# Pairwise adds and residual adds as accumulating DMAs in a fused attention and GeGLU block

## The chip, the cores and the metric

The kernel runs on one core of a Trainium2 chip. The metric is the device time of one execution in microseconds (us). Three executions of the kernel before gave 184.48, 184.34 and 184.0 us, so a median of 184.34 us.

## What is computed

The input is a bf16 activation x of 2048 rows (tokens) and 512 columns. The output is x plus the output of an attention branch plus the output of a feed-forward branch, both fed with a layer norm of x that has no scale or bias.

```
xn  = layernorm(x)                                   # 2048 x 512
q, k, v = xn @ wqkv                                  # 32 heads of 16 columns each
logit[h, s, w] = sum_d q[h,s,d] * k[h,s-2w,d] / 4    # w = 0..7, a dilated window of 8 keys
attn = softmax over w (keys before the start masked)
o[h, s, d] = sum_w attn[h,s,w] * v[h,s-2w,d]
out = x + o @ wo + (gelu(xn @ w_gate) * (xn @ w_up)) @ w_down      # 1376 inner columns
```

## The kernel before

The 2048 tokens are cut into four blocks of 512. In the code they have the numbers b = 0 to 3; the text calls them block one to block four. Tokens also come in sixteen tiles of 128 rows, four to a block. Activations are held transposed: a partition is a column of x, and the 512 tokens of a block lie along the free axis. Columns of wqkv are picked with a stride, so that a partition holds four groups (g = 0 to 3) of 512 tokens, and the 16 columns of one head are spread over four neighbouring partitions and the four groups.

For each block the work goes through these steps.

1. Layer norm of the block's tiles. For blocks one and two VectorE does it with ScalarE's square root; for blocks three and four ScalarE does the sums, GpSimd a power (L832, one operation for two tiles) and VectorE a reciprocal (L803). Blocks two to four are transposed by DMA transposes from SyncE's queue (L882, called SP in the profile).
2. Projections on TensorE, 128x512 matmuls in groups of four: q, k and v (L1009, names mm), gate and up (L1217, names fg and fu). ScalarE moves the results out of PSUM, with the tanh form of GELU for the gate.
3. Logits. VectorE multiplies q with eight shifted views of k: four products of 128x4096, one for each group (L1040, names pr). Two adds of 128x4096 (L1053, names pa) bring them to two: product 0 + 1, and product 2 + 3. The rest of the sum over d is done by TensorE against a matrix E8 that adds four partitions and scales: the task er (L1073 to L1094), which also holds 16 small matmuls for the last up columns (L1078). For both remaining products it issues 8 matmuls (L1085), four of which side by side fill the four 32-row strips of a PSUM bank.
4. Softmax over the window. VectorE takes the maximum (L1117) and subtracts it (L1122), ScalarE the exponential (L1131), VectorE sums, takes the reciprocal (L1138 to L1150) and multiplies (L1155). The probabilities go to a scratch in HBM by four stores (L1164) and come back spread over the partitions of a head by four loads (L1176).
5. Values. VectorE makes four products of 128x4096 (L1184, names pv), three adds (L1193, names pw) and a last add of the two halves (L1199, name pz), which gives the transposed attention output.
6. Feed-forward. VectorE multiplies the GELU with the up projection (L1241 and L1279, names h).
7. Output, for each tile of 128 tokens: 4 matmuls with wo and 11 with w_down into one bank (L1302, names acc). For tiles 0 to 13 ScalarE copies the bank to an SBUF buffer OB (L1335, names fe), VectorE adds the tile of x (L1340, names fin), which SP had loaded into a buffer XR (L1288, names ldxr), and SP stores OB (L1353, names sto). The last two tiles are cut into two and three column parts, and VectorE adds from PSUM (L1346). There are two XR and four OB buffers.

Every instruction or DMA is a task of a graph, with what it reads and writes. The dictionary ORDER (L404 to L461) writes out by hand, for each of the five engines, in which order its tasks are issued. The function schedule (L207) replays these orders with assumed durations, only to hand out buffers of the pools; assign_sync (L317) gives each task a semaphore and finds the waits; emit_engine (L364) issues the tasks in the order written. Each engine works strictly in its order, so a task at the head that waits holds up all behind it.

The parts that the change touches: PR_ADD3 (L512) is empty in the kernel before. For blocks that it names, a third pairwise add is made at L1060 to L1063, and the reduction issues the E8 matmuls for one product only (hhs at L1071, L1082). The tuple FIN2 (L511) names the tiles of step 7 that take ScalarE's copy and VectorE's residual add from SBUF.

Of the kernel before, what the change touches and what calls it, by code (L numbers as in the profile page):

```python
# [12 lines left out]
    DMA_ISSUE=0.48,  # L13
    DMA_FIXED=2.0,
# [5 lines left out]
    DRAIN=0.1,  # L20
# [115 lines left out]
class Graph:  # L136
# [70 lines left out]
    def schedule(self, orders, params=None):  # L207
# [59 lines left out]
        for _ in range(len(self.tasks)):  # L267
# [23 lines left out]
            elif t.eng == "pe":  # L291
                sw = 0.0
                if t.mode is not None:
                    if pe_mode not in (None, t.mode):
                        sw = prm["PE_MODE_SWITCH"]
                    pe_mode = t.mode
                t.end = est + sw + pe_clock.run(est, t.dur, t.util)
                t.done = t.end + prm["PE_DRAIN"]
            else:
                t.end = est + t.dur  # L300
                t.done = t.end + prm["DRAIN"]
                if t.eng == "act" and t.table is not None:
                    act_table = t.table
# [13 lines left out]
    def assign_sync(self, cnt_sems, dma_sems):  # L317
        order = self.order
        for e in ("pe", "act", "dve", "pool"):
            for i, t in enumerate(order[e]):  # L320
                t.seq = i + 1
                t.sem = cnt_sems[e]
                t.val = i + 1
        dcount = [0] * len(dma_sems)
        dlast = [None] * len(dma_sems)
        k = 0
        for t in order["sp"]:
# [6 lines left out]
            dlast[si] = t  # L334
        self.dma_totals = [(dma_sems[i], dcount[i]) for i in range(len(dma_sems)) if dcount[i] > 0]
        know = {e: {} for e in ENGS}
        allt = sorted((t for t in self.tasks if not t.dropped), key=lambda t: (t.start, t.idx))
        for t in allt:
            K = know[t.eng]
            deps = list(t.deps)  # L340
            if t.eng == "sp" and t.prev_on_sem is not None:
                deps.append(t.prev_on_sem)
# [21 lines left out]
    def emit_engine(self, eng_name, e):  # L364
# [7 lines left out]
        for t in self.order[eng_name]:  # L372
# [4 lines left out]
            if eng_name == "sp" and t is self.order["sp"][-4]:  # L377
                late = self.order["sp"][-7:]
                for (s, tot) in self.dma_totals:
# [3 lines left out]
            ins.then_inc(t.sem, 16 if eng_name == "sp" else 1)  # L383
# [5 lines left out]
    def report(self):  # L389
# [17 lines left out]
        "warm14 mma0_0 tpx0_1 mmt0_0 mmt0_1 mmt1_0 tpx1_0 mmt1_1 mmt0_2 tpx1_1 mmt1_2 mmt0_3 mmt1_3 "  # L407
        "mm0_2_0_0 mm0_2_3_0 mm0_2_2_0 mm0_2_1_0 fg0_0 fg0_1 fg0_2 fu0_0 fg0_3 fu0_1 fu0_2 fg0_4 fu0_3 fg0_5 "
        "fu0_4 fu0_5 fg0_6 fg0_7 er0_3 mm1_0_0_0 mm1_1_0_0 mm1_0_1_0 mm1_1_1_0 fg1_0 fu0_6 mm1_0_3_0 "
        "mm1_0_2_0 mm1_1_3_0 fu0_7 fu1_0 fg1_1 fg0_8 fu1_1 mm1_1_2_0 fu0_8 mm1_2_0_0 fg1_2 fg0_9 fu1_2 "  # L410
        "mm1_2_2_0 fg1_3 fu1_3 fu0_9 fg0_10 fg1_4 fu1_4 mm1_2_3_0 fg1_5 mm1_2_1_0 fg1_6 fu1_5 fu1_6 fg1_7 "
        "mm2_0_0_0 mm2_1_1_0 mm2_1_0_0 mm2_0_3_0 er1_3 mm2_0_1_0 fg1_10 mm2_1_2_0 mm2_2_1_0 mm2_0_2_0 fu1_7 "
        "fg2_0 accd1 mm2_1_3_0 accd2 fg2_1 mm2_2_3_0 mm2_2_2_0 fg1_8 fg2_2 acca0 fu2_0 accb0 fg1_9 mm2_2_0_0 "
        "accd3 er2_3 fu2_1 fu1_8 fu1_9 fu2_2 fg2_3 fu2_3 mm3_1_2_0 mm3_1_1_0 mm3_1_3_0 mm3_0_1_0 mm3_0_0_0 "
        "fg2_4 mm3_1_0_0 fu2_4 mm3_0_2_0 fg3_0 mm3_0_3_0 fu3_0 fg3_1 fg2_10 fg3_2 accd7 accd5 mm3_2_0_0 "
        "fg2_5 fu3_1 fg3_3 mm3_2_3_0 mm3_2_1_0 fu2_5 fu3_2 acca4 er3_3 accb4 fg3_4 accd6 fu3_3 fu3_4 fg2_6 "
        "fg3_5 fu2_6 fg2_7 fg3_6 fu2_7 fg2_8 fu2_8 fu3_5 fg3_7 fu3_6 mm3_2_2_0 fg2_9 fu3_7 fu2_9 fg3_8 fu3_8 "
        "fg3_9 fg3_10 acca8 accd10 accd9 fu3_9 accb8 accd11 acca12 accd13 accd14_0 accd14_1 accw14_0 "
        "accw14_1 accw13 accb12 accd15_0 accw12 accw15_0 accd15_1 accw15_1 accd15_2 accw15_2",
    "act":  # L420
        "c_tbl sx1 sq0 negm1 sxx1 sq1 evx0_0 evx0_1 evq0_0 sq2 evq0_1 evk0_0 evx1_0 sq3 evk0_1 bnst8 evx1_1 "
        "bnst9 evq0_2 sq6 evk0_2 evq0_3 evk0_3 ve8 evv0_0_0 sq4 vp8 bnag8 bnag9 va8 gelu0_0 evv0_2_0 "
        "evv0_3_0 bnst10 gelu0_1 bnst11 uev0_2 gelu0_3 vb8 gelu0_4 uev0_1 uev0_3 ve10 gelu0_5 uev0_4 uev0_0 "
        "uev0_5 gelu0_2 halo1 vp10 gelu0_7 bnag10 bnag11 evq1_0_0 evk1_0_0 evv0_1_0 evq1_1_0 evk1_1_0 "
        "gelu0_6 exp0 sub11 evq1_3_0 evk1_3_0 evq1_2_0 va10 uev0_7 uev1_0 uev0_10c uev0_6 sub9 vb10 sub8 "
        "uev1_1 evk1_2_0 norm9 uev0_10b gelu1_1 gelu1_0 norm8 gelu0_8 evv1_0_0 gelu1_2 sub10 uev0_8 bnst12 "
        "gelu0_9 norm11 uev1_2 uev0_9 norm10 evv1_2_0 gelu1_4 gelu1_3 uev1_3 evv1_1_0 uev1_4 uev1_5 uev0_10a "
        "bnst13 gelu1_5 gelu0_10 uev1_6 evk2_1_0 evv1_3_0 evk2_0_0 ve12 vp12 gelu1_7 bnag12 evq2_0_0 gelu1_6 "
        "evq2_1_0 uev1_10b bnag13 uev1_10c halv1 evk2_2_0 evq2_2_0 halo2 exp1 bnst14 sub12 bnst15 uev1_7 "
        "va12 ve14 vb12 uev1_10a vp14 bnag14 evk2_3_0 bnag15 evq2_3_0 evv2_1_0 va14 vb14 fe1 fe2 sub14 "  # L430
        "gelu2_0 evv2_2_0 halo3 gelu1_10 sub15 uev2_0 norm12 sub13 evv2_0_0 evv2_3_0 norm13 fe0 norm15 fe3 "
        "norm14 gelu1_8 gelu2_1 gelu1_9 uev2_1 uev1_8 uev2_2 uev1_9 uev2_3 gelu2_2 evk3_2_0 evk3_1_0 "
        "uev2_10b gelu2_3 exp2 evq3_1_0 evk3_3_0 evq3_2_0 evq3_0_0 halv2 evk3_0_0 uev2_10c evq3_3_0 uev2_4 "
        "uev2_10a gelu2_10 gelu3_1 uev3_0 gelu3_0 fe7 evv3_0_0 gelu2_5 gelu3_3 evv3_1_0 uev2_5 uev3_1 fe5 "
        "gelu2_4 gelu3_2 uev3_10c halv3 evv3_3_0 uev3_2 fe4 fe6 uev3_3 uev3_10b exp3 gelu3_5 uev2_6 gelu3_4 "
        "gelu2_7 uev2_7 uev2_8 gelu3_6 gelu2_6 evv3_2_0 gelu3_7 uev3_4 gelu2_8 gelu2_9 uev2_9 uev3_10a "
        "uev3_7 uev3_5 uev3_6 gelu3_10 fe10 gelu3_8 gelu3_9 uev3_9 fe9 uev3_8 fe8 fe11 fe13 fe12",
    "dve":
        "c_wdz bnst0 bnag0 sub0 rstd0 norm0 mean1 sub1 evy0_0 rstd1 norm1 evy0_1 bnst2 bnag2 sub2 rstd2 "
        "norm2 bnst3 bnag3 sub3 rstd3 norm3 bnst7 bnst6 bnst5 bnag6 bnag7 bnst4 bnag5 sub7 rstd6 bnag4 sub6 "  # L440
        "norm7 sub4 sub5 norm6 pr0_2 pr0_0 pr0_3 rstd4 pr0_1 norm4 norm5 pa0_1 pa0_0 h0_0 h0_1 h0_2 mask "
        "d1_0 d2_0 pr1_0 pr1_1 d4a_0 d4b_0 d4c_0 d5_0 rstd8 d6_0 pr1_3 pa1_0 pr1_2 h0_3 pa1_1 pv0_1 rstd10 "
        "pv0_3 h0_4 pv0_0 h1_1 pv0_2 pw0_1 h0_10 pw0_2 d1_1 pw0_3 d2_1 pz0 pr2_2 d4a_1 pr2_0 d4b_1 h1_3 "
        "d4c_1 h1_2 d5_1 h1_0 d6_1 pr2_1 pr2_3 pa2_0 fin1 rstd12 pa2_1 h1_10 pv1_1 rstd14 pv1_3 d1_2 pv1_0 "
        "d2_2 pv1_2 pw1_1 fin3 pw1_2 h2_1 pw1_3 h1_4 d4a_2 pz1 d4b_2 pr3_1 d4c_2 pr3_2 d5_2 fin0 d6_2 pr3_3 "
        "pr3_0 h2_0 h2_10 pa3_0 fin2 pa3_1 pv2_0 pv2_2 d1_3 pv2_1 d2_3 pw2_1 h3_1 d4a_3 h3_0 d4b_3 fin7 "
        "d4c_3 h2_2 d5_3 fin5 d6_3 pv2_3 pw2_2 h2_3 pw2_3 h2_4 pz2 fin4 pv3_3 pv3_0 pv3_1 fin6 pw3_1 fin10 "
        "h3_3 h3_10 pv3_2 h3_2 fin9 h3_4 pw3_2 fin8 pw3_3 fin11 pz3 fin14_0 fin14_1 fin13 fin15_0 fin15_1 "
        "fin12 fin15_2",
    "pool":  # L450
        "c_ones c_onef c_id c_vnpad c_idb c_eps c_mhalf c_e8a c_e8b c_e8c c_e8d c_ktpad c_mask0 c_mask1 "
        "c_utz sq8 sq10 sq12 sq14",
    "sp":
        "ld_x0_0 ld_x0_1 ld_wq ld_x1_0 ld_wk ld_x1_1 ld_wv ld_x2 ld_x4 ld_x3 ld_wg0 ld_wu0 ld_wt0 ld_x5 "
        "ld_wt1 trx3_0 ld_wt2 trx3_1 trx2_0 trx2_1 ld_wd0 ld_x6 ldxr1 ld_x7 ld_wd1 ld_wo ss0_2 ss0_3 ss0_0 "
        "ss0_1 ldxr2 sl0_1 sl0_3 sl0_2 trx4_0 sl0_0 trx4_1 trx5_1 trx5_0 ss1_2 ss1_3 ss1_1 ss1_0 sl1_1 sl1_3 "
        "sl1_0 sl1_2 ldxr3 trx6_0 trx6_1 trx7_1 trx7_0 sto3 sto1 ldxr0 ldxr7 ss2_1 ss2_2 ss2_3 ss2_0 sl2_0 "
        "sl2_3 sl2_2 sto0 sl2_1 sto2 ldxr5 ldxr4 sto5 ss3_0 ss3_1 ss3_2 ss3_3 ldxr10 sl3_3 sl3_0 sl3_2 sl3_1 "
        "ldxr6 sto4 sto6 ldxr8 ldxr9 sto9 ldxr11 ldxr14 sto8 sto7 sto10 ldxr13 sto11 sto14_0 sto14_1 ldxr15 "
        "ldxr12 sto13 sto15_0 sto15_1 sto12 sto15_2",  # L460
# [20 lines left out]
def bass_parallel_sum__sliding_local_dilated__glu_gated_geglu__prompt_kernel(nc, A_x, A_wqkv, A_wo, B_x, B_w_gate, B_w_up, B_w_down, out, dbg=None, cfg=None):  # L481
# [28 lines left out]
    PPOW = cfg.get("PPOW", 4)  # L510
    FIN2 = cfg.get("FIN2", tuple(range(14)))  # L511
    PR_ADD3 = cfg.get("PR_ADD3", ())  # L512
# [11 lines left out]
    with contextlib.ExitStack() as es:  # L524
# [56 lines left out]
        cnt = {e: es.enter_context(nc.semaphore("cnt_" + e)) for e in ("pe", "act", "dve", "pool")}  # L581
        dsems = [es.enter_context(nc.semaphore("dma%d" % i)) for i in range(NDMASEM)]
# [360 lines left out]
        for b in range(NB):  # L943
# [94 lines left out]
            for g in range(4):  # L1038
# [21 lines left out]
                if g == 3 and b in PR_ADD3:  # L1060
                    t_of["pa%d_2" % b] = G.task(
                        "dve", "pa%d_2" % b, d_dve(4096, 0.52), mk_pa(pr_items[0], pr_items[2]),
                        rd=[pr_items[2]], wr=[pr_items[0]], prio=base + 20.2)  # L1063
# [218 lines left out]

            for ti in range(4):
                t = 4 * b + ti
                it_xr = Item("xr%d" % t, P_xr, "xr")

                def mk_xr(t=t, it=it_xr):
                    return lambda e: e.dma_start(XR[:, it.slot, :], x2[128 * t:128 * t + 128, :])  # L1288
                t_xr = G.task("sp", "ldxr%d" % t, 0, mk_xr(), wr=[it_xr], prio=base + 58, nbytes=128 * 1024)
                G.order_after(t_xr, t_of["gelu%d_5" % b])  # L1290
# [47 lines left out]

# [78 lines left out]
```

## Time and profile before

| what | value |
|---|---|
| median of three runs | 184.34 us |
| the profiled execution: its own time | 184.58 us |
| the profiled execution: its span in the profile | 182.7 us |
| granted TensorE clock | 1.0 throughout |
| third pairwise add of the logit products | none |
| L1085 reduction matmuls | 64, 16 in each block |
| L1340 residual adds, 128x512 | 14, mean 416 ns |
| L1053 pair adds, 128x4096 | 8, mean 2286 ns |
| DMAs from GpSimd | none |

The profile is of one execution. PE is TensorE's matmuls and PEld its weight loads, DVE is VectorE, ACT is ScalarE, POOL is GpSimd, SP is SyncE, SPq the issuing of DMAs on its queue. The chain of work is followed back from the last instruction, at each step to what released it or to the instruction before it on its engine; each piece has a start, a length, and the engine and line. A timeline has a start, a length, the engine and line, the operation, output and input tiles, and at the end, in brackets, idle time before it and what ended it. Durations overlap: a VectorE operation begins before the one ahead has drained, so what an operation costs its engine is read from start to start. In a table of stretches each engine has its busy time and instructions in the stretch, then come the granted clock, the mean busy share of the 16 DMA engines and the GB/s that they moved.

### The profile page before, as it was taken

The page shows a single profiled execution, that of the slowest core. Times are in us where ns is not written, and L with a number is a line of the kernel's source. Part 1 is how long each engine was busy: PE and PEld are TensorE (multiplying, and loading weights), DVE is VectorE, ACT ScalarE, POOL GpSimd, SP SyncE. Part 2 cuts the span into 40 slices and gives each one's busy share as a digit, 9 for nine tenths or more (in the row PEclk, how much of TensorE's full clock was granted, in tenths as well). Part 3 has the DMA queues.
Part 4 walks back from the last instruction along what each step waited for, and adds up shares of the span by engine and source line. Part 5 has one row for each costly group of instructions (what it writes and reads, how often), then busy time and mean ns, then how long its engine had stood idle before and what let it go on. Part 6 is the DMA issues. An engine that isn't in the chain of part 4 may idle for free.

```text
span 182.7 us, 2790 instructions
## 1 busy us (share of the span) xinstructions
PE 178.9 (98%) x1068; PEld 90.6 (50%) x1068; DVE 169.6 (93%) x172; ACT 128.4 (70%) x258; POOL 9.5 (5%) x23
## 2 busy tenths in 40 slices
PE   8999999999999999999999999999999999999994
PEld 2886444544444444444444544444444444444664
DVE  3769999999999999999999999999999999999922
ACT  5688987999999899998695977527449764234011
POOL 6000010003300000122000000000000000000000
PEclk9999999999999999999999999999999999999999
DMA  4999905932562000002851020128000346022433
GB/s 125 360 376 381 125 18 118 367 127 49 183 145 57 0 0 4 0 12 76 256 62 30 4 82 0 30 62 285 28 0 0 92 131 213 0 86 61 140 104 100
DMA packets 26221, 19.60 MB, mean 107 GB/s; under 512 B 13825, under 2 KB 23009, under 8 KB 26209
## 3 DMA queue, kind: packets, MB, share of 16 engines
q1 hardware_dynamic: 26208, 19.44, 37.0%
q8 instruction: 8, 0.13, 0.3%
q14 instruction: 5, 0.03, 0.1%
HBM read 14.71 MB, written 3.15 MB: 98 GB/s over the span
## 4 chain that ended last, share of the span: by engine, by line
PE 91%; DMA 4%; SPq 2%; ACT 1%; issue 0%; DVE 0%; DVEq 0%
PE PS L1217 38%; PE PS L1302 28%; PE PS L1009 19%; DMA XIN<-in_A_x_dram 4%; PE PS L1256 2%; PE PS L1085 2%; PE PS L1078 1%; PE PS L959 1%; SPq L731 1%; SPq L687 1%; ACT XS L769 0%; SPq L737 0%; ACT xnT L919 0%; DVE OB L1346 0%; DVEq L376 0%
## 5 line engine op out<-in xcount | busy, mean ns | idle before, releaser
L1302 PE MATMUL PS<-Wd,HT 128*128 128x512 bf16 (+2 forms) x209 | 41.0, 346 | 0.0
L1217 PE MATMUL PS<-xnT,Wg 128*128 128x512 bf16 x160 | 39.8, 379 | 0.0
L1217 PE MATMUL PS<-xnT,Wu 128*128 128x512 bf16 x160 | 39.1, 379 | 0.0
L1009 PE MATMUL PS<-xnT,Wqkv 128*128 128x512 bf16 x160 | 38.0, 380 | 0.0
L1184 DVE TENSOR_TENSOR UNI<-VN,PT 128x4096 f16<-128x4096 bf16 x16 | 36.3, 2287 | 0.0
L1040 DVE TENSOR_TENSOR UNI<-QT,KT 128x4096 f16<-128x4096 bf16 x16 | 36.1, 2286 | 0.0
L1302 PEld LDWEIGHTS PS<-Wd,HT 128*128 128x128 bf16 x209 | 19.6, 98 | 19.2 <-issue 0.4
L1234 ACT ACTIVATE UU<-PS 128x512 bf16<-128x512 f32 x40 | 23.1, 600 | 6.4 <-PE PS L1217 6.1
L1193 DVE TENSOR_TENSOR UNI<-UNI 128x4096 f16<-128x4096 f16 x12 | 27.5, 2290 | 0.0
L1227 ACT ACTIVATE GG<-PS 128x512 bf16<-128x512 f32 x40 | 22.9, 602 | 5.9 <-DVE HT L1241 5.8
L1009 PEld LDWEIGHTS PS<-xnT,Wqkv 128*128 128x128 bf16 x160 | 17.9, 113 | 16.9 <-issue 0.8
L1217 PEld LDWEIGHTS PS<-xnT,Wu 128*128 128x128 bf16 x160 | 15.6, 98 | 19.0 <-ACT XIN L853 0.4
L1217 PEld LDWEIGHTS PS<-xnT,Wg 128*128 128x128 bf16 x160 | 15.7, 98 | 18.7
L1335 ACT ACTIVATE OB<-PS 128x512 bf16<-128x512 f32 x14 | 8.3, 601 | 17.3 <-PE PS L1302 15.1
L1053 DVE TENSOR_TENSOR UNI<-UNI 128x4096 f16<-128x4096 f16 x8 | 18.2, 2286 | 0.0
L1302 PE MATMUL PS<-Wo,OT 128*128 128x512 bf16 (+2 forms) x76 | 16.5, 346 | 0.0
L1020 ACT ACTIVATE VN<-PS 128x512 bf16<-128x512 f32 x16 | 9.3, 597 | 6.5 <-PE PS L1009 6.5
L1241 DVE TENSOR_TENSOR HT<-GG,UU 128x1024 bf16<-128x1024 bf16 x20 | 13.6, 686 | 0.0
L832 POOL TENSOR_TENSOR sq<-ve,mhalf 128x2 bf16<-128x2 f32 x4 | 6.6, 1657 | 72.8 <-ACT ve L828 72.8
L1302 PEld LDWEIGHTS PS<-Wo,OT 128*128 128x128 bf16 x76 | 7.1, 98 | 6.6 <-issue 0.3
L1272 ACT ACTIVATE UT<-PS 64x256 bf16<-64x256 f32 (+1 forms) x12 | 5.4, 447 | 6.7 <-PE PS L1256 3.9
L959 PE MATMUL PS<-xnT,Wqkv 128*128 128x128 bf16 x128 | 8.3, 222 | 0.3 <-ACT xnT L919 0.2
(85 smaller groups left out, 159.5 us busy)
## 6 DMA issues: line engine op xcount, KB each, us to landing
PT<-pt_scratch SPq DMA_DIRECT2D x16, 256.0 KB, 4.2
XR<-in_A_x_dram SPq DMA_DIRECT2D x16, 128.0 KB, 2.2
out_dram<-OB SPq DMA_DIRECT2D x14, 128.0 KB, 1.9
Wqkv<-in_A_wqkv_dram SPq DMA_DIRECT2D x3, 512.0 KB, 5.0
XIN<-in_A_x_dram SPq DMA_DIRECT2D x6, 256.0 KB, 6.7
Wg<-in_B_w_gate_dram SPq DMA_DIRECT2D x1, 1280.0 KB, 8.6
Wu<-in_B_w_up_dram SPq DMA_DIRECT2D x1, 1280.0 KB, 11.6
Wd<-in_B_w_down_dram SPq DMA_DIRECT2D x1, 1280.0 KB, 6.6
```

Of the source, the lines that this page charges most:

```text
L959: ins = e.matmul(PS[:, 512 * it.slot + 128 * g:512 * it.slot + 128 * g + 128], lhsT=wcols(which, kt, g), rhs=xnT[:, itx.slot, kt, t * 128: ...
L1009: ins = e.matmul(PS[:, 512 * it.slot:512 * it.slot + 512], lhsT=wcols(which, kt, g), rhs=xnT[:, itx.slot, kt, :], start=(kt == 0), stop=(k ...
L1020: return e.activation(out=o, in_=PS[:, 512 * it.slot:512 * it.slot + 512], func=ACTF.Identity, scale=(QSC, 1.0, 1.0)[which])
L1040: return lambda e: e.tensor_tensor(out=UNI[:, it.slot, :, :], in0=bass.AP(QT, (itq.slot * 4 + g) * 512, [[NQT * 4 * 512, 128], [0, 8], [1, ...
L1053: return lambda e: e.tensor_tensor(out=UNI[:, i0.slot, :, :], in0=UNI[:, i0.slot, :, :], in1=UNI[:, i1.slot, :, :], op=ALU.add)
L1184: return lambda e: e.tensor_tensor(out=bass.AP(UNI, ito.slot * 4096, [[NUNI * 4096, 128], [2048, 2], [512, 4], [1, 512]]), in0=bass.AP(VN, ...
L1193: return lambda e: e.tensor_tensor(out=UNI[:, i0.slot, :, :], in0=UNI[:, i0.slot, :, :], in1=UNI[:, i1.slot, :, :], op=ALU.add)
L1217: ins = e.matmul(PS[0:M, 512 * it.slot:512 * it.slot + 512], lhsT=Wx[:, kt, j * 128:j * 128 + M], rhs=xnT[:, itx.slot, kt, :], start=(kt = ...
L1227: return lambda e: e.activation(out=GG[:, ito.slot, q, :], in_=PS[:, 512 * it.slot:512 * it.slot + 512], func=ACTF.Gelu_apprx_tanh)
L1234: return lambda e: e.activation(out=UU[:, ito.slot, q, :], in_=PS[:, 512 * it.slot:512 * it.slot + 512], func=ACTF.Identity)
L1241: return lambda e: e.tensor_tensor(out=HT[:, ito.slot, j - 1:j + 1, :], in0=GG[:, ig.slot, :, :], in1=UU[:, iu.slot, :, :], op=ALU.mult)
L1302: ins = e.matmul(PS[:, 512 * it.slot:512 * it.slot + CW], lhsT=(OT[:, ito.slot, q, ti * 128:(ti + 1) * 128] if kind == "o" else HT[:, ith. ...
```

## The change

- PR_ADD3 becomes (1, 2, 3): in blocks two, three and four the third pairwise add is made, so that one product is left, and the reduction on TensorE issues 8 matmuls of L1085 in place of 16.
- That third add is no VectorE operation: it is a DMA issued from GpSimd (names pd1, pd2, pd3) that adds one 1 MiB SBUF tile onto another (128 partitions x 4096 fp16). The reduction waits for it.
- A new tuple FIN3 names tiles 0 to 7, the tiles of blocks one and two. For these the residual is no longer loaded into XR and added by VectorE: one DMA on SP's queue for each of the two blocks copies 512 rows of x to the output in HBM (names prx0, prx1), and for each tile a DMA from GpSimd adds OB onto those rows (names sta0 to sta7). They stand in the place of the eight loads, adds and stores.
- The eleven DMAs from GpSimd use six semaphores of their own, in turn; each waits for the one six before it. SP waits for the last of them ahead of its last stores.
- The orders of all five engines in ORDER are written anew. TensorE has the same 186 tasks as before and VectorE 164 in place of 172. On GpSimd the order after the constants is: power, power, pd1, power, power, pd2, sta0, sta2, sta3, sta1, sta4, pd3, sta5, sta7, sta6. SP issues 86 DMAs in place of 100.

Cut to its core, without the new text of ORDER:

```diff
-    def assign_sync(self, cnt_sems, dma_sems):
+    def assign_sync(self, cnt_sems, dma_sems, acc_sems):
...
+        last = [None] * len(acc_sems)
+        for k, t in enumerate(q for q in order["pool"] if q.nbytes):
+            i = k % len(acc_sems)
+            t.sem = acc_sems[i]
+            t.val = 16 * (k // len(acc_sems) + 1)
+            t.prev_on_sem = last[i]
+            last[i] = t
+        self.acc_last = [t for t in last if t is not None]
...
+                for q in self.acc_last:
+                    e.wait_ge(q.sem, q.val)
...
+    FIN3 = cfg.get("FIN3", tuple(range(8)))
     FIN2 = cfg.get("FIN2", tuple(range(14)))
-    PR_ADD3 = cfg.get("PR_ADD3", ())
+    PR_ADD3 = cfg.get("PR_ADD3", (1, 2, 3))
...
+        asems = [es.enter_context(nc.semaphore("acc%d" % i)) for i in range(6)]
...
                 if g == 3 and b in PR_ADD3:
-                    t_of["pa%d_2" % b] = G.task(
-                        "dve", "pa%d_2" % b, d_dve(4096, 0.52), mk_pa(pr_items[0], pr_items[2]),
-                        rd=[pr_items[2]], wr=[pr_items[0]], prio=base + 20.2)
+                    def mk_pd(i0=pr_items[0], i1=pr_items[2]):
+                        return lambda e: e.dma_start(UNI[:, i0.slot, :, :], UNI[:, i1.slot, :, :], accum_op=ALU.add,
+                                                     max_dma_last_dim=4096)
+                    t_of["pa%d_2" % b] = G.task("pool", "pd%d" % b, 1.5, mk_pd(), rd=[pr_items[2]], wr=[pr_items[0]],
+                                                prio=base + 20.2, nbytes=1024 * 1024)
...
+            if 4 * b in FIN3:
+                def mk_px(b=b):
+                    return lambda e: e.dma_start(out2[512 * b:512 * b + 512, :], x2[512 * b:512 * b + 512, :])
+                t_px = G.task("sp", "prx%d" % b, 0, mk_px(), wr=[(I_out, b)], prio=base + 58, nbytes=512 * 1024)
+                G.order_after(t_px, t_of["gelu%d_5" % b])
...
+                        if t in FIN3:
+                            def mk_ao(t=t, ito=it_ob):
+                                return lambda e: e.dma_start(out2[128 * t:128 * t + 128, :], OB[:, ito.slot, :],
+                                                             accum_op=ALU.add,
+                                                     max_dma_last_dim=4096)
+                            G.task("pool", "sta%d" % t, 1.5, mk_ao(), rd=[it_ob, (I_out, t // 4)], prio=base + 62,
+                                   nbytes=128 * 1024)
+                            continue
```

## The prediction

> **What bounds the kernel now.** First the page's busy times and its chain of work, then the chain in order of time, which shows whether the leading engine ever stands still.
>
> ```profile
> span 182.7 us, 2790 instructions
> PE 178.9 (98%) x1068; PEld 90.6 (50%) x1068; DVE 169.6 (93%) x172; ACT 128.4 (70%) x258; POOL 9.5 (5%) x23
> PE 91%; DMA 4%; SPq 2%; ACT 1%; issue 0%; DVE 0%; DVEq 0%
> 12.90 1.98 PE PS L959 x32
> ...
> 65.05 0.55 PE PS L1078 x16
> 65.60 0.86 PE PS L1085 x16
> ...
> 93.35 0.55 PE PS L1078 x16
> 93.90 0.86 PE PS L1085 x16
> ...
> 129.19 0.55 PE PS L1078 x16
> 129.74 0.86 PE PS L1085 x16
> ...
> 163.52 16.75 PE PS L1302 x122
> 180.26 0.03 issue
> ```
>
> From 12.90 to 180.26 us the pieces follow each other with one gap of 0.23 us (before block one's reduction): TensorE is the bound as long as it is fed, and an instruction taken off it shortens the run by its own step. The L1085 pieces are the reductions of the logit products, 16 matmuls in 0.86 us, so 0.054 us each. VectorE, at 93%, has little room and works just ahead. Its timeline gives the ends of the last pair add (L1053) of blocks two, three and four, and, start to start, what each operation costs: 2.20 us for 128x4096, 0.60 for the 128x1024 multiply, 0.34 for the 128x512 residual add (L1340).
>
> ```profile
> 49.28 2.29 DVE L1053 TENSOR_TENSOR UNI<-UNI 128x4096 f16<-128x4096 f16 x1
> 51.48 2.29 DVE L1184 TENSOR_TENSOR UNI<-VN,PT 128x4096 f16<-128x4096 bf16 x1
> ...
> 87.08 0.42 DVE L1340 TENSOR_TENSOR OB<-OB,XR 128x512 bf16<-128x512 bf16 x1
> 87.42 0.16 DVE L803 RECIPROCAL rstd<-sq 128x2 f32<-128x2 bf16 x1
> 87.49 2.27 DVE L1053 TENSOR_TENSOR UNI<-UNI 128x4096 f16<-128x4096 f16 x1
> ...
> 125.53 2.29 DVE L1053 TENSOR_TENSOR UNI<-UNI 128x4096 f16<-128x4096 f16 x1
> ```
>
> Last, the DMA engines in stretches (the two columns at the end are their busy share and GB/s). At 91 to 99 us four transposes run: little moved, yet 40 to 48% busy.
>
> ```profile
> 53.00:57.00 4.00, 4.00 (x20) 1.90 (x19) 4.00 (x5) 3.62 (x8) 0.00 (x0) 1.00 0.49 113
> 91.00:95.00 4.00, 4.00 (x45) 1.83 (x44) 3.74 (x4) 3.66 (x8) 0.00 (x0) 1.00 0.48 80
> 95.00:99.00 4.00, 4.00 (x20) 1.79 (x19) 4.00 (x3) 2.78 (x7) 0.00 (x0) 1.00 0.40 36
> ```
>
> **What the Trainium skill says.** "DMA: Bandwidth & Descriptors", section "Anatomy of one DMA — SWDGE (gpsimd) path", prices a DMA from GpSimd at about 2.0 us plus bytes / 436e3. "Collectives: The Full Stack", section "The bandwidth ceiling: the fold count and why AG ≠ RS ≠ AR", says an add inside a DMA needs two source reads, and that these, not the add, cost time. The trace of before has no such DMA; both are unconfirmed here. "DMA: Bandwidth & Descriptors", section "Issuing engines are not separate DMA queues": all queues share the same 16 engines. "SBUF — State Buffer", section "Who interferes with whom": a VectorE operation with two SBUF inputs holds the read interface it shares with GpSimd, while descriptor writing needs the write interface (called an inference). The trace agrees on reads: GpSimd's power (L832) takes 0.71 to 2.84 us for the same 128x2.
>
> **The change, part by part.**
>
> TensorE loses 8 of 16 reduction matmuls in blocks two, three and four: 24 x 0.054 = 1.29 us. Nothing is added to it. A group below means four 128x512 matmuls, 0.8635 us (3.45 / 4).
>
> VectorE loses eight residual adds: 8 x 0.34 = 2.7 us. It is not on the chain, so I count nothing directly; it makes the last add of block four earlier.
>
> New wait: the reduction, at the head of TensorE's in-order queue, waits for the accumulating DMA, and the whole stream stands behind it. The room is from the end of the second pair add to the time at which TensorE gets there.
> - Block two. The VectorE operations ahead of its add are the same as before: it ends at 49.28 + 2.29 = 51.6. TensorE leaves the first reduction at 32.12 and has 40 groups ahead of the next: 32.12 + 34.5 = 66.7. Room 15.1.
> - Block three. Against before, one residual add and one reciprocal (0.07) leave, one 128x512 multiply (0.34) enters, and a wait of 0.24 us for the reduction goes, since the maximum now stands behind one more 2.20 us add. The add ends at 89.76 - 0.3 = 89.5. TensorE: 66.7 + 0.98 (0.55 + 0.43, the shorter reduction) + 22 groups (19.0) + 60 output matmuls (12.96) = 99.6. Room 10.1.
> - Block four. Three residual adds (1.02), one 128x1024 and one 128x512 multiply (0.94) leave its stretch, a reciprocal enters: 127.82 - 0.3 - 1.9 = about 125.3, after a short wait for the third reduction. TensorE: 99.6 + 0.98 + 28 groups (24.2) + 45 output matmuls (9.7) = 134.5. Room 9.2.
>
> Price of that DMA (1 MiB), from add to release. One read by the formula: 2.0 + 2.4 = 4.4; two reads: 6.8. From the trace: a 128 KB store lands in 1.9 us and a 32 KB one in 1.5, so about 1.4 fixed; Wd's 1280 KB take 6.6, so 5.2 for 1.31 MB, 4.2 for 1.05 MB, 8.3 read twice: 9.7 in all. To each I add an estimated 1 us for GpSimd's issue: 5.4 to 10.7. I take 7.8 (two reads by the formula), because SBUF to SBUF need not run at the speed of an HBM load. That fits all rooms by 1.4 us or more.
>
> Sharing. The second DMA runs at 90 to 98 beside the transposes for block four. Their share is 0.48 x 4 + 0.40 x 4 = 3.5 us of all engines. If it waits for half of that it takes 9.6, inside 10.1; if for all, 11.3, a stall of 1.2. The first runs beside the transposes for block three (0.49 of 4 us), but has 15 us; those must land by TensorE's first use of them at 32.12 + 35 groups = 62.4, and SP issues the last near 57. I take no stall and keep up to 1 us for the range.
>
> GpSimd. The first and second DMAs wait for VectorE's adds; behind them stand the power of block four (at 76.8, long after 51.6) and four output stores nobody needs soon. The third stands behind the fifth output store, which needs its TensorE sum: 99.6 + 1.0 + 17 groups + 30 matmuls = 121.8, plus 0.6 for ScalarE's copy; 2.9 us ahead of 125.3, more than any GpSimd step seen. Cost nothing; if an issue takes over 2.9 us, the excess falls on the third DMA.
>
> SP loses eight residual loads and eight stores, gains two 512 KB copies. The first comes where a residual load stood at 30.4 us, behind weights and 11 us ahead of the first probability store at 42.2; the second near 59, with 20 us to the next store at 80.6. Wo's load moves back behind the first probability loads; its first use is after 71. Nothing, hidden by those distances.
>
> What is late next. The fourth reduction moves from 129.2 to 134.5, so the softmax of block four starts later, but its chain on VectorE is packed: maximum, subtraction, the table load and exponential on ScalarE, sums, reciprocal and product, 1.14 + 1.13 + 1.28 + 1.02 + 0.73 + 0.87 + 0.60 = 6.8 plus some 1.2 of handovers, from 135.5 to 143.5, about where it ended before (143.6). Then come four products, three adds, three multiplies and four residual adds: 152.0 + 19.4 = 171.4, and TensorE needs the result at 173.74 - 1.29 = 172.45. Spare 1.0 us; the cost is nothing.
>
> Sum: the profiled execution took 184.58 us (span 182.7 and 1.9 around it); 184.58 - 1.29 = 183.29. It lies 0.24 above the median of 184.34, so against that the time is 183.05, say 183.1.
>
> The orders of all engines are rewritten, so ScalarE's evacuations of PSUM and TensorE's refills meet in new places. ScalarE is 70% busy and the order of before keeps TensorE fed to 0.23 us, so I take nothing for this, and up to 0.5 us for the range.
>
> **The rivals.** *The accumulating DMA becomes the bound (slower).* With T its time and half the transposes' share (1.75) on block three's, the stalls are (T - 9.2) + (T + 1.75 - 10.1); they eat the 1.29 us at T = 9.4, without sharing at 10.3. At the upper price of 10.7: 1.5 + 2.35 = 3.9, so 184.34 - 1.29 + 3.9 = 186.9; unshared 1.5 + 0.6 = 2.1, so 185.2. For it: twice-read bytes at the trace's load rate, two reductions with under 2 us to spare. Against: the formula. Chance 0.27, centre 186.
>
> *The gain is given back by sharing (same).* Block three's DMA waits for the whole 3.5 us: 1.2 us, 184.3. For it the 40 to 48% share, against it the light traffic. Chance 0.13.
>
> *GpSimd and VectorE hold each other up (slower).* If each of eleven issues cost VectorE 1 us, less about 2 us of room (1.0 spare, some of the 2.7 removed): 9 us, 192. The inference on the write interface speaks against it. Chance 0.03.
>
> *The plan holds (faster)*: chance 0.57, own range 182.6 to 183.6.
>
> **How the numbers follow.** 0.3% is 0.55 us, about what a measurement of this kernel tells from no change: faster 0.57, same 0.13, slower 0.30. The low end is the full gain with half a microsecond of spread in the runs (184.0 to 184.48). The high end takes in the slow DMA nearly to its shared price, and leaves out one in ten above.
>
> **What would show it.** Right: reduction pieces of 0.43 us, no idle TensorE before any, the accumulating DMA landing in 7 to 9 us, VectorE's L1340 group at 6. Wrong: TensorE idle before the third or fourth reduction on a GpSimd DMA (slow accumulate); idle before block three's or four's first projection on a transpose (sharing); 128x4096 operations far over 2.29 us (shared interface).

## The result and the profile after

The changed kernel is slower: 189.97 us (median of 4 runs, 189.72 to 190.42) against 184.41 us for the kernel before on the same chip (4 runs), a ratio of 1.0305 with a 95% interval of 1.0287 to 1.0324. The forecast of 183.1 us missed by 6.9; the result lies even above 186.9, the time of the slow-DMA rival at its upper price. Medians here and below are of all runs, while the ratios leave out single runs far above the rest of their kernel, so that the two can differ a little. The profiled execution took 190.08 us, its span is 188.4, and its mean granted TensorE clock is 0.991 where it was 1.0.

First the page of the changed kernel (span, busy times, the shares of the chain by engine), then the chain of work in order of time around blocks three and four.

```profile
span 188.4 us, 2732 instructions
PE 179.4 (95%) x1044; PEld 90.1 (48%) x1044; DVE 167.9 (89%) x164; ACT 128.0 (68%) x258; POOL 19.9 (11%) x34
PE 59%; DVE 22%; DMA 12%; ACT 3%; SPq 1%; issue 1%; DVEq 0%
```

```profile
55.84 7.39 DMA xnT<-XIN
...
67.78 0.55 PE PS L1091 x16
68.33 0.43 PE PS L1098 x8
...
101.20 4.59 DMA xnT<-XIN
...
132.29 9.30 DMA UNI<-UNI
141.64 0.62 PE PS L1091 x16
```

TensorE's part of the change is there: the reduction (now L1098) takes 0.43 us where it took 0.86. But DMA has 12% of the chain where it had 4%. Of its three long pieces here, two are the DMA transposes xnT<-XIN of blocks three and four. The third is block four's accumulating DMA (UNI<-UNI), which does release its reduction, but TensorE had hardly come to it. TensorE's timeline gives the idle time in brackets: there is none ahead of a reduction, and some ahead of the first projections (L1020) of blocks three and four.

```profile
63.28 1.92 PE L1020 MATMUL PS<-xnT,Wqkv 128*128 128x512 bf16 x8 [1.35 <-DMA xnT<-XIN]
105.88 7.79 PE L1020 MATMUL PS<-xnT,Wqkv 128*128 128x512 bf16 x28 [4.06 <-DMA xnT<-XIN]
```

Next SP's timeline: start and length of issuing block four's four transposes, before (first line, 7.25 us, in part waiting for the norms) and after.

```profile
89.23 7.25 SPq L882 DMA_TRANSPOSE xnT<-XIN  x4
```

```profile
91.94 10.57 SPq L893 DMA_TRANSPOSE xnT<-XIN  x4
```

Last the table of stretches of the changed kernel around that gap (start and end, length, busy time and instructions of PE, PEld, DVE, ACT and POOL, then granted clock, share of the DMA engines, GB/s), and two lines on its DMAs: all that GpSimd issued (packets, MB, share of the engines' span), and the pair-add DMA's median time from issue to landing.

```profile
91.00:95.00 4.00, 4.00 (x20) 1.82 (x19) 4.00 (x3) 3.91 (x9) 2.64 (x4) 1.00 0.75 131
95.00:99.00 4.00, 4.00 (x21) 1.88 (x19) 4.00 (x2) 2.72 (x6) 0.69 (x1) 1.00 1.03 160
99.00:103.00 4.00, 2.81 (x33) 1.18 (x31) 3.45 (x3) 2.95 (x7) 0.84 (x1) 1.00 1.25 183
...
107.00:109.00 2.00, 2.00 (x6) 0.73 (x5) 0.62 (x2) 1.17 (x3) 0.00 (x0) 0.50 0.00 0
```

```profile
q0 software_dynamic: 1968, 4.20, 14.3%
...
UNI<-UNI POOLq DMA_DIRECT2D x3, 1024.0 KB, 9.3
```

From 91 to 99 us, where the engines were 48 and 40% busy before, they are now 75 and 103% busy (packets overlap in time, so a share can pass 1), and from 99 to 103 us, where they were idle, 125%. Then the clock: from 107 to 109 us it is 0.50, and TensorE gets 6 matmuls done in 2 us.

The account: gaps of 1.35 and 4.06 us. After the second one the 28 projections take 7.79 us, where the same 28 take 6.23 in the first experiment below, with the clock at full: 1.56 lost. Less the reductions' 1.29, 1.35 + 4.06 + 1.56 - 1.29 = 5.68 us, against 190.08 - 184.58 = 5.50 between the two profiled executions. One run below puts the rest of the change at -0.3.

### The profile page after: what moved, and what is told of

Same layout as the page of the kernel before. It is cut to its first block, busy times and chain, and to the rows that moved or that the text cites. A ratio compares the mean times of both kernels' runs of the same rounds, so it can differ in the third digit from the quotient of the medians.

```text
span 188.4 us, 2732 instructions
## 1 busy us (share of the span) xinstructions
PE 179.4 (95%) x1044; PEld 90.1 (48%) x1044; DVE 167.9 (89%) x164; ACT 128.0 (68%) x258; POOL 19.9 (11%) x34
## 3 DMA queue, kind: packets, MB, share of 16 engines
q0 software_dynamic: 1968, 4.20, 14.3%
## 4 chain that ended last, share of the span: by engine, by line
PE 59%; DVE 22%; DMA 12%; ACT 3%; SPq 1%; issue 1%; DVEq 0%
PE PS L1321 22%; PE PS L1230 20%; PE PS L1020 10%; DVE UNI L1051 9%; DMA xnT<-XIN 6%; DMA UNI<-UNI 5%; DVE UNI L1064 5%; PE PS L970 4%; DVE UNI L1206 1%; DVE UNI L1197 1%; DMA XIN<-in_A_x_dram 1%; PE PS L1091 1%; DVE rc L1163 1%; PE PS L1098 1%; PE PS L1269 1%
## 5 line engine op out<-in xcount | busy, mean ns | idle before, releaser
L1020 PE MATMUL PS<-xnT,Wqkv 128*128 128x512 bf16 x160 | 39.3, 391 | 5.4 <-DMA xnT<-XIN 5.4
L1230 PE MATMUL PS<-xnT,Wg 128*128 128x512 bf16 x160 | 38.9, 379 | 0.0
L1197 DVE TENSOR_TENSOR UNI<-VN,PT 128x4096 f16<-128x4096 bf16 x16 | 36.0, 2284 | 1.1 <-DMA PT<-pt_scratch 1.1
L1020 PEld LDWEIGHTS PS<-xnT,Wqkv 128*128 128x128 bf16 x160 | 17.9, 115 | 24.0 <-issue 6.8
L1206 DVE TENSOR_TENSOR UNI<-UNI 128x4096 f16<-128x4096 f16 x12 | 27.4, 2286 | 0.0
L1240 ACT ACTIVATE GG<-PS 128x512 bf16<-128x512 f32 x40 | 23.4, 602 | 3.4 <-PE PS L1230 3.3
L1064 DVE TENSOR_TENSOR UNI<-UNI 128x4096 f16<-128x4096 f16 x8 | 18.1, 2284 | 0.0
L1360 POOL DMA_DIRECT2D out_dram<-OB x8 | 7.9, 1086 | 49.7 <-ACT OB L1354 49.7
L1031 ACT ACTIVATE KT<-PS 128x512 bf16<-128x512 f32 x12 | 7.2, 596 | 6.4 <-PE PS L1020 6.4
```

Of the source, the lines that this page charges most:

```text
L1020: ins = e.matmul(PS[:, 512 * it.slot:512 * it.slot + 512], lhsT=wcols(which, kt, g), rhs=xnT[:, itx.slot, kt, :], start=(kt == 0), stop=(k ...
L1031: return e.activation(out=o, in_=PS[:, 512 * it.slot:512 * it.slot + 512], func=ACTF.Identity, scale=(QSC, 1.0, 1.0)[which])
L1064: return lambda e: e.tensor_tensor(out=UNI[:, i0.slot, :, :], in0=UNI[:, i0.slot, :, :], in1=UNI[:, i1.slot, :, :], op=ALU.add)
L1197: return lambda e: e.tensor_tensor(out=bass.AP(UNI, ito.slot * 4096, [[NUNI * 4096, 128], [2048, 2], [512, 4], [1, 512]]), in0=bass.AP(VN, ...
L1206: return lambda e: e.tensor_tensor(out=UNI[:, i0.slot, :, :], in0=UNI[:, i0.slot, :, :], in1=UNI[:, i1.slot, :, :], op=ALU.add)
L1230: ins = e.matmul(PS[0:M, 512 * it.slot:512 * it.slot + 512], lhsT=Wx[:, kt, j * 128:j * 128 + M], rhs=xnT[:, itx.slot, kt, :], start=(kt = ...
```

## The experiments

Three theories stood at the start. A: the pair-add DMAs, beside block three's and four's transposes, take the DMA engines from them. B: the output accumulates (sta) that follow pd2 do it. C: the rewritten orders start the transposes too late (91.94 instead of 89.23 us). Each kernel is the changed kernel with the edit shown; times are medians, and ratios are to the kernel before on the same chip (184.2 to 184.5 us in these comparisons).

**No pair-add DMA.** PR_ADD3 is empty and pd1 to pd3 leave GpSimd's order; the output accumulates and the new orders stay.

```diff
-    PR_ADD3 = cfg.get("PR_ADD3", (1, 2, 3))
+    PR_ADD3 = cfg.get("PR_ADD3", ())
```

> The three pair-add DMAs are taken out and the reduction issues 16 matmuls again in every block; the new orders, the residual copies and the eight output accumulates stay. Theory A (the pair-add DMAs fill the DMA engines, so the transposes for blocks three and four land late and TensorE stands still): no TensorE gap over 0.5 us before a first projection, transposes landing in about 3 us, and the 1.29 us of matmuls come back: 184.0 to 184.9 us. Theory B (the output accumulates and residual copies load the DMA engines): a gap of 3 us or more before block four's first projection stays, 188 to 190. Theory C (the new order alone starts the transposes too late): the gap of 4 us stays too, 189 to 191.

Measured 183.9 us, ratio 0.9983 (0.9969 to 0.9997), no gap before block three's or four's projections. SP's timeline of this kernel, then TensorE's at block four's first projections:

```profile
91.58 5.18 SPq L893 DMA_TRANSPOSE xnT<-XIN  x4
```

```profile
101.82 6.23 PE L1020 MATMUL PS<-xnT,Wqkv 128*128 128x512 bf16 x28
```

The transposes start as late as in the changed kernel, are issued in half the time, and nobody waits. C falls, and so does B alone. The residual part of the change with the new orders is worth -0.3 us, with an interval that nearly reaches 0. The page also gives the size of an output accumulate, since they are now all that GpSimd issues:

```profile
q0 software_dynamic: 1152, 1.05, 4.7%
```

4.7% of 183.0 us is 8.6 us of all 16 engines for eight, 1.07 us each for 128 KB.

**Output accumulates later.** sta0 to sta3 wait for block four's last transpose.

```diff
+        by_name = {q.name: q for q in G.tasks}
+        for q in range(4):
+            G.order_after(by_name["sta%d" % q], by_name["trx7_0"])
         G.schedule(ORDER, SCHED)
```

> All as in the changed kernel, but the first four output accumulates wait until the last transpose for block four has landed. Theory A: the gap before block four's first projection stays at 3 us or more, since 1 MiB of pair add weighs more than four times 128 KB: 188.5 to 190 us. Theory B: the gap goes, 184 to 185.5. Theory C: nothing changes, 190.

Measured 186.31 us, ratio 1.0095 (1.0065 to 1.0125), with one of the four runs at 193.69: the numbers of A missed, and so did those of B. In the profiled execution block three's gap stayed at 1.60 us, block four's fell from 4.06 to 1.92, the slow matmuls were not there, and issuing the transposes took 8.59 us. The line has the gap in brackets; "issue" means that the profile names nothing that TensorE waited for.

```profile
104.15 6.21 PE L1020 MATMUL PS<-xnT,Wqkv 128*128 128x512 bf16 x28 [1.92 <-issue]
```

So, with pd2 ahead of them, the accumulates that "nobody needs soon" carry about half of block four's gap; without the pair-add DMAs they had made none. From here A reads: the DMA engines are asked for more than they have while transposes run, by pd2 and by the output accumulates behind it.

**Copies in place of the pair-add DMAs.** The same DMA without its add: the same bytes from the same place to the same place. This kernel leaves the third pair add out of the result.

```diff
-                        return lambda e: e.dma_start(UNI[:, i0.slot, :, :], UNI[:, i1.slot, :, :], accum_op=ALU.add,
+                        return lambda e: e.dma_start(UNI[:, i0.slot, :, :], UNI[:, i1.slot, :, :],
```

> The three pair-add DMAs become plain copies of the same tiles from GpSimd (the third pair add is left out of the result). Theory A with the second read as the price: each lands in about 5 us in place of 8.4 to 10.9, the gaps before the projections shrink to under 2 us in all, 183.5 to 186 us. If the price is GpSimd's path or SBUF to SBUF itself and not the add: 8 us or more and 189 to 190 as in the changed kernel. Theories B and C: 189 to 190.

Measured 182.84 us, ratio 0.9914 (0.9894 to 0.9935), and in the profiled execution (span 181.1 us) no gap before any matmul after the first 14 us. GpSimd's DMAs:

```profile
q0 software_dynamic: 1968, 4.20, 9.4%
...
UNI<-UNI POOLq DMA_DIRECT2D x3, 1024.0 KB, 6.0
```

Here is the forecast gain, with the orders and the waits as in the changed kernel; what stood in its way is what an accumulate costs more than a copy. The q0 lines give it, if the output accumulates' 8.6 us are the same in all kernels: (14.3% x 188.4 - 8.6) / 3 = 6.1 us of all 16 engines for a 1 MiB accumulate, (9.4% x 181.1 - 8.6) / 3 = 2.8 for the copy. It lands in 9.3 us instead of 6.0 (medians).

**Pair-add DMA in blocks two and four only.** PR_ADD3 = (1, 3), pd2 leaves the order.

```diff
-    PR_ADD3 = cfg.get("PR_ADD3", (1, 2, 3))
+    PR_ADD3 = cfg.get("PR_ADD3", (1, 3))
```

> Only block three's pair-add DMA is taken out (its reduction has 16 matmuls again); those of blocks two and four stay. Theory A: the 4.06 us gap before block four's first projection and the slow clock behind it go, the 1.35 us gap before block three's stays: 184.4 - 0.86 + 1.35 = 184.9, so 184.4 to 185.5 us. Theories B and C: the 4 us gap stays, 189 to 190.5.

Measured 184.67 us, ratio 1.0012 (0.9995 to 1.003), single runs from 183.39 to 192.46; in the profiled one, of 183.66 us, block four's gap is gone and block three's is 0.59, where A had expected 1.35 to stay. For block four A holds, and pd2 is the one pair-add DMA behind its gap. The transposes are issued as without any, in 5.20 us.

**Wo's load later.** For block three the suspect beside pd1 is a load of 0.5 MB that the new order puts ahead of its last transposes.

```diff
-        "sl0_1 trx4_0 sl0_0 sl0_3 sl0_2 ld_wo trx4_1 trx5_0 trx5_1 prx1 ss1_1 ss1_2 ss1_0 ss1_3 sl1_0 sl1_1 "
+        "sl0_1 trx4_0 sl0_0 sl0_3 sl0_2 trx4_1 trx5_0 trx5_1 ld_wo prx1 ss1_1 ss1_2 ss1_0 ss1_3 sl1_0 sl1_1 "
```

> The changed kernel with one move: on SP's queue Wo's load (0.5 MB) goes from ahead of the second transpose of block three to behind the fourth. Theory A (transposes are late because the DMA engines are asked for more than they have in that stretch): in block three's stretch Wo's load is some 2 us of all engines, so its gap of 1.35 us shrinks to 0.3 or less, block four's of 4.06 us stays, and the time falls by 1.1 to 1.4, to about 188.7. Rival D (block three's transposes are late because of the accumulate alone): gap of 1.35 stays, 190.

Measured 188.81 us, ratio 1.0233 (1.019 to 1.0277). As A expected: block three's gap is gone, and block four's stays, with slow matmuls behind it again.

```profile
61.72 4.48 PE L1020 MATMUL PS<-xnT,Wqkv 128*128 128x512 bf16 x20
...
104.49 7.68 PE L1020 MATMUL PS<-xnT,Wqkv 128*128 128x512 bf16 x27 [4.26 <-DMA xnT<-XIN]
```

**Both moves.** Wo's load later and the four output accumulates later, all three pair-add DMAs kept (both edits as above).

> The changed kernel with all three pair-add DMAs and both moves (Wo's load behind block three's last transpose; the first four output accumulates after block four's last transpose). Theory A: each move takes away its own piece, and what is left is the accumulate of block three beside block four's transposes: the version with the output accumulates late had gaps of 1.6 and 1.92 us and took 186.3, so with Wo's load moved the first gap goes: 184.7 to 185.0, one gap of about 1.9 us before block four's first projection. Rival (the pieces are not independent; block four's transposes only move): 186 or more.

Measured 184.65 us, ratio 1.0012 (0.9987 to 1.0038). As expected: no gap at block three, one of 2.06 us at block four.

```profile
102.25 6.21 PE L1020 MATMUL PS<-xnT,Wqkv 128*128 128x512 bf16 x28 [2.06 <-issue]
```

The pieces nearly add up: the moves give back the first gap (1.35), half of the second (2.0) and the slow matmuls (1.56), together 4.9 of 189.97 - 184.65 = 5.3. What remains is pd2 beside the transposes, about 2 us, against which the 1.29 us of TensorE and the 0.3 of the residual part come out at nothing.

**Both moves, no pd2.** The same with PR_ADD3 = (1, 3).

> The kernel without block three's pair-add DMA (184.7 us median, 0.59 us of gap left before block three's first projection, runs from 183.4 up), with two moves: Wo's load behind block three's last transpose, and the first four output accumulates held until block four's last transpose has landed. Theory A: nothing big lies beside either block's transposes, so no gap is left and two reductions of 0.43 in place of 0.86 us are gained: 184.4 - 0.86 = 183.5, with a narrower spread. Rival (what was left there came from the accumulates of blocks two and four themselves): 184.4 to 184.7 and as wide.

Measured 183.25 us (22 runs), ratio 0.9956 (0.9939 to 0.9974): A holds for the time. The spread did not narrow as far as expected: 17 of 22 lie between 182.7 and 184.0, five above. The chain of this kernel by engine, from its page:

```profile
PE 94%; DMA 3%; issue 1%; ACT 1%; SPq 0%; DVE 0%; DVEq 0%
```

TensorE is the chain again. This is the fastest version that computes everything: under the kernel before by 1.1 us in the medians and 0.8 by the ratio, where 16 matmuls less are worth 0.86 and the residual part 0.3.

**All operations kept, orders rearranged.** The orders are changed so that fewer big transfers lie beside the transposes; the core of it, in SP's, VectorE's and GpSimd's orders:

```diff
-prx0 ss0_1 ss0_3 ss0_2 ss0_0 sl0_1 trx4_0 sl0_0 sl0_3 sl0_2 ld_wo trx4_1 trx5_0 trx5_1 prx1
+ss0_3 ss0_1 ss0_2 ss0_0 trx4_1 sl0_2 sl0_1 sl0_0 trx4_0 sl0_3 trx5_0 trx5_1 prx0 prx1 ld_wo
...
-d5_1 h1_3 d6_1 pa2_0 pr2_3 pr2_2 h1_10 pa2_1 rstd14 rstd12 pv1_0 pv1_1 pv1_2
+d5_1 rstd12 d6_1 pr2_2 pr2_3 pa2_0 pa2_1 pv1_2 pv1_1 rstd14 h1_2 pv1_0
...
-pd2 sta0 sta2 sta3 sta1 sta4 pd3 sta5 sta7 sta6
+pd2 sta1 sta2 sta0 sta7 pd3 sta5 sta4 sta3 sta6
```

> All the changed kernel's operations, with the five orders rearranged so that the DMA engines have room where transposes run: Wo's load behind block three's transposes, both row copies there too, the power and reciprocals of block four's layer norm earlier so that its transposes start about 2 us earlier, the first output accumulates later, block four's first projections one group later. Theory A: the collisions go and the full 1.29 us is there: no gap over 0.3 us on TensorE before any projection, 182.8 to 183.6. Rival (accumulating DMAs cost more than their collision with the transposes, for instance by holding VectorE or the reduction): 184.3 or more, with gaps in front of the reductions.

Measured 183.96 us (22 runs, 182.54 to 185.27), ratio 0.9965 (0.9944 to 0.9985), between the two expectations. No projection waits for a transpose, but the runs differ by 2.7 us, and the chain is no longer TensorE's:

```profile
DVE 71%; PE 16%; DMA 8%; issue 2%; SPq 2%; DVEq 0%
```

**The same without block three's pair-add DMA.**

> The rearranged version of the changed kernel (183.96 us median, runs from 182.5 to 185.3) without block three's pair-add DMA; TensorE does that block's 16 matmuls again. Theory A: block three's accumulate (6 us of all engines) is what makes its runs differ, so the spread shrinks to under 1 us, and 0.43 us of TensorE come back: 183.3 to 183.6. Rival (the spread comes from VectorE, which works without room in this order): spread as before, 184.0 to 184.4.

Measured 184.42 us, ratio 0.9989 (0.9971 to 1.0006), 183.12 to 185.91: the rival holds. pd2 is not what makes these runs differ; VectorE has 68% of the chain here too. Against the kernel with pd2, 184.42 - 183.96 = 0.46 us, which would be the 0.43 of its reduction. But the two intervals overlap and the chain is VectorE's, so that pd2 pays here what was forecast is not shown; it does no visible harm.

**Another rearrangement**, with both row copies behind block four's transposes.

> All the changed kernel's operations in another rearrangement: like the first one, but with both row copies behind block four's transposes, only three output accumulates ahead of the last pair-add DMA, and block three's reduction one group later. Theory A: 183.0 to 184.0, gap of at most 0.3 us before any projection; rival (VectorE without room sets the time in such orders): 184 or more with TensorE waiting for VectorE.

Measured 184.33 us, ratio 0.9996 (0.9984 to 1.0008). A's numbers missed; no projection waits for a transpose, but TensorE waits 0.47 us for ScalarE ahead of block two's reduction, and the chain is 63% TensorE and 26% VectorE. So late transposes are not what kept it from A's numbers; what did stays open.

**The clock.** Do the slow matmuls come from the gap? Theory E says that a gap of some 4 us makes the granted clock fall to half for about 3 us. Two kernels without pair-add DMAs (183.9 us, no gap), with a gap made by holding block four's last two transposes, or the last one, until block three's reduction on TensorE.

```diff
+        by_name = {t.name: t for t in G.tasks}
+        G.order_after(by_name["trx6_0"], by_name["er2_3"])
         G.schedule(ORDER, SCHED)
```

> The kernel without pair-add DMAs (183.9 us, no gap), with block four's last two transposes held until TensorE has finished block three's reduction near 101.8 us. They land near 106.6, a gap of about 4.8 us before the first projection, with nothing else on the DMA engines. Theory E (a gap of some 4 us makes the granted clock fall to half for about 3 us): 8 matmuls at 0.43 us after it, 1.7 us more, 190.4. Rival (the slow matmuls of the changed kernel had another cause than the gap): 188.7, all matmuls at 0.216 us.

> As the one before, but only block four's last transpose is held until 101.8 us. It lands near 105.3: a gap of about 3.5 us. Theory E has seen no slow matmuls after 1.92 us and 3 us of them after 4.06, so this says on which side 3.5 lies: 187.4 with no slow matmuls, 189.1 with them. Rival (gap is not the cause): 187.4 here and no slow matmuls after the longer gap either.

The diff is that of the long gap; for the middle one trx7_0 stands in the place of trx6_0. The long gap: two runs, 188.21 us at a mean clock of 1.0 and 189.47 at 0.990. The middle one: 186.34 at 1.0 and 187.86 at 0.991. The profiled execution with the long gap, in the timeline and in the stretch behind it:

```profile
105.57 5.99 PE L1020 MATMUL PS<-xnT,Wqkv 128*128 128x512 bf16 x27 [4.07 <-DMA xnT<-XIN]
```

```profile
107.00:109.00 2.00, 2.00 (x11) 1.02 (x9) 0.31 (x1) 1.83 (x5) 0.00 (x0) 1.00 0.00 0
```

A gap of 4.07 us with the clock at 1.0 and 11 matmuls in 2 us, where the changed kernel had 6 after 4.06. Theory E fell as it was put: the length of a gap does not settle it. But with a gap and no pair-add DMA, one run of two had a lower clock in both kernels, while the twelve runs of the same kernel without the gap kept 0.999 or more. That a gap makes it likelier fits these few runs; they don't show that it is needed. Lower clocks turn up in runs that were not profiled, with gaps unknown: one of four with the output accumulates later (193.69 us at 0.982), three of twenty without pd2 (187.09 to 192.46 us, 0.982 to 0.991), one of 22 with both moves and no pd2 (188.34 us at 0.991), and one of 124 of the kernel before (186.48 us at 0.991). The Trainium skill, "TensorE: Matmul & The Clock Gate", section "Part 1: The HAM clock gate (the "warmup" mystery)", describes a free-running window over which activity is judged and says that results differ from run to run for that reason. That fits, and these runs do not show the window itself. In the changed kernel all four runs were at 0.982 or 0.991, and so were all four with Wo's load later. The mean clock alone doesn't give the loss: the changed kernel's two runs at 0.982 were no slower (189.72 and 189.86 us) than the two at 0.991 (190.08 and 190.42).

## Why the prediction was wrong

The transposes' issue on SP's queue and the gap behind it, over all kernels with these orders:

| kernel | issue of block four's transposes, us | gap before its first projection, us | median, us |
|---|---|---|---|
| no pair-add DMA | 5.18 | 0 | 183.9 |
| blocks two and four only | 5.20 | 0 | 184.67 |
| both moves, no pd2 | 5.16 | 0 | 183.25 |
| copies | 7.33 | 0 | 182.84 |
| output accumulates later | 8.59 | 1.92 | 186.31 |
| both moves | 8.74 | 2.06 | 184.65 |
| changed kernel | 10.57 | 4.06 | 189.97 |
| Wo's load later | 10.53 | 4.26 | 188.81 |

Up to some 7 us there is room; between 8.6 and 10.6 us, each microsecond of issue is about one of TensorE.

By the prediction's steps:

- *TensorE loses 1.29 us*: right. L1098 has 40 matmuls, its pieces 0.43 us, and the version with copies is 1.6 us faster than before (1.29 and the 0.3 of the residual part).
- *VectorE loses eight adds, off the path*: right, the group is at 6.

```profile
L1098 PE MATMUL PS<-UNI,E 128*32 128x512 f16 x40 | 2.9, 379 | 0.0
L1368 DVE TENSOR_TENSOR OB<-OB,XR 128x512 bf16<-128x512 bf16 x6 | 2.4, 421 | 0.8 <-ACT OB L1354 0.8
```

- *The new wait and its rooms*: right in its outcome. In block two the second add's end was put at 51.6 and TensorE's arrival at 66.7; they are 51.1 and 67.78, of which 1.35 is the gap. No reduction waits by more than about 0.2 us, although block four's is released by its DMA (132.29 + 9.30 = 141.59). There it was in part luck: from the end of the add at 132.0 to the release it took 9.6 us, more than the forecast room of 9.2, and the prediction's own terms for that add, 127.82 - 0.3 - 1.9, give 125.6 and not 125.3, so a room of 8.9.
- *Price of that DMA, 7.8 us*: too low, 9.3 from issue to landing (8.4 to 10.9). It cost next to nothing where it was looked for, before the reductions. The statement of the Trainium skill that it rests on ("Collectives: The Full Stack", section "The bandwidth ceiling: the fold count and why AG ≠ RS ≠ AR": an add inside a DMA needs two source reads), made there for collectives, fits the engine time, 6.1 us against 2.8 for a copy; the reads themselves no run shows.
- *Sharing*: this step failed. It asked what the transposes do to the pair-add DMA (9.6 or 11.3 us) and never priced what the DMA does to the transposes. The DMA took 8.4 us beside block four's transposes, no longer than the other two took (10.9 and 9.3); it was the transposes that waited, for it and for the output accumulates behind it, and they cost TensorE 4.06 us. The sentence with the needed bound was written ("those must land by TensorE's first use of them at 32.12 + 35 groups = 62.4, and SP issues the last near 57"), for block three, and closed with "I take no stall and keep up to 1 us for the range"; the stall was 1.35. For block four the same line was not drawn at all: the first use comes right behind the reduction, at about 100.6 in the prediction's own count, and the transposes, issued until 96.5 before, had some 4 us of room.
- *GpSimd, "four output stores nobody needs soon"; SP, "Wo's load moves back"; cost nothing*: right on who waits for them, wrong on whom they hold up. The output accumulates take 1.07 us of all engines each, four of them 4.3 us, and stand right behind pd2; together with pd2 they made block four's gap, about half of which goes when they are moved. Wo's load, together with pd1, made block three's: in the kernels that leave out pd1 or move the load there is none.
- *What is late next* and *ScalarE's new meeting places*: nothing was lost there; the version with copies has no gap.
- Not in the prediction: a gap can be followed by matmuls at half the clock, 1.56 us here.

Of the rivals, "the accumulating DMA becomes the bound" did not come: no reduction waits for long. "Given back by sharing" had the right two parties, with the victim the wrong way round and a fifth of the size. "GpSimd and VectorE hold each other up" did not come: VectorE's 128x4096 pair adds take 2284 ns on the mean, 2286 before. The prediction's own list of what would show it wrong had the case: TensorE idle before block three's or four's first projection on a transpose.

What the engine time leaves out. The sum of what is asked of the engines from pd2's issue to the first use orders most kernels (changed: 6.1 + 4.3 + 3.5 = 13.9 us; without pd2 7.8), but not two of them: with copies it is 2.8 + 4.3 + 3.5 = 10.6 and nobody waits, with the accumulate alone 6.1 + 3.5 = 9.6 and there is a gap of 1.9. So an accumulate delays its neighbours by more than its engine time. The queues in the traces show how: block four's transposes waited for nearly the whole of the big transfer, not for a share of it. First the changed kernel from 92.4 to 98 us, while pd2 ran (q0 is GpSimd's queue, q1 SP's; packets, MB, share of the engines; then the transposes issued and their median time to landing), second the copy from 91 to 94 us, third the stretch behind it, 94 to 99.2 us.

```profile
q0 software_dynamic: 234, 0.96, 103.5%
q1 hardware_dynamic: 8, 0.00, 0.3%
...
xnT<-XIN SPq DMA_TRANSPOSE x3, 8.7
```

```profile
q0 software_dynamic: 272, 1.00, 100.4%
```

```profile
q1 hardware_dynamic: 2176, 0.52, 63.1%
```

With three transposes issued, SP's queue got 8 packets through in 5.6 us; in the kernel without pair-add DMAs it was 1921 from 92 to 98 us. Beside the copy it got none, and 2176 in the stretch behind it. But the copy was over at 94 us, while the accumulate still ran at 98. Block three's transposes were held less completely: 121 packets from 57 to 61 us beside pd1.

What stays open. Why GpSimd's packets went ahead, no run here tells, and whether a pair-add DMA cut into pieces would let the transposes through was not run. Nor was it settled why the runs of the rearranged kernels differ by up to 2.8 us, or when a gap is followed by the lower clock.

## What to carry to other kernels

When a transfer is added, list what else is in flight on the DMA engines until the next due time of anybody, and cost the delay of the neighbours, not only the delay of the new transfer: a few small transposes ahead of the leading engine were the first to pay here. Transfers that nobody waits for still take engine time; put them, and weight loads with late first use, behind the ones with a due time. A big DMA can hold small ones back for nearly its whole length, so price their delay at that length. Here, once Wo's load and the output accumulates were out of the way, two of the three pair-add DMAs paid; the third, beside the transposes, cost a gap of 2.06 us, more than the 1.29 that all three gave.

## What the runs showed of the hardware

- A 1 MiB SBUF to SBUF accumulate from GpSimd took 6.1 us of all 16 DMA engines in the changed kernel (5.3 to 6.3 over the kernels with it, worked out in the same way), 2.8 as a plain copy; it took between 8.5 and 9.5 us from issue to landing (medians of the kernels with them), 6.0 as a copy. A 128 KB accumulate onto HBM took 1.07 us of all engines.
- Four transposes that moved little (36 to 80 GB/s) took 3.5 us of all engines before, and their issue on SP's queue backs up when the engines are busy: 5.2 us for four in the quiet kernels, 10.6 beside the accumulates.
- While a 1 MiB DMA from GpSimd ran, block four's transposes on SP's queue moved next to nothing, 8 packets in 5.6 us beside an accumulate and none in 3 us beside a copy, and ran after it; block three's got 121 packets through in 4 us.
- TensorE's clock fell to half for about 3 us behind gaps of 4.06 and 4.26 us, and not behind one of 4.07 (each in one profiled execution).
